# Declaring that operations on the two different banks of a two-bank PSUM tile need not wait for each other

## The chip, the core and the metric

The kernel runs on one core of a Trainium2 chip. The metric is the device time of one execution in microseconds (us). The kernel before was run three times: 1634.38, 1642.93 and 1643.38 us, with a median of 1642.93 us. One further execution was profiled; it took 1644.29 us.

## What is computed

The kernel computes eight batches of sigmoid attention and, on its result, a mixing step and a two-layer network with a ReLU between the layers. Cut to what matters, with B = 8 batches, 12 heads of 64, a sequence of S = 448, d_model = 768 and rank 32:

```python
scores = np.matmul(q, k.transpose(0, 1, 3, 2)) / np.sqrt(64) - np.log(S)
attn = 1.0 / (1.0 + np.exp(-scores))
x = np.matmul(attn, v)                   # heads put side by side: B x S x 768
u = x + (x.transpose(0, 2, 1) @ U @ V).transpose(0, 2, 1)
out = u + np.maximum(u @ w_ch1, 0.0) @ w_ch2
```

The two weight matrices come as 64-bit floating-point numbers and are decoded on the chip.

## The kernel before, in words

**Stages.** A pair of heads at a time, the scores of a pair are computed on TensorE (line L520), put through the sigmoid on ScalarE (L615), split into two float16 parts (L635 on ScalarE, L381 on VectorE) and multiplied by the values (L531, L535); L641 takes the result out of PSUM. Line L381 is a helper (`stt`), so many VectorE operations carry it, those that add a PSUM result to a tile in SBUF among them. After the attention of a batch come the mixing (L686 to L727 for the first two batches, L779 and L788 for the later ones) and the network. Float32 operands are held as two float16 parts, and three products stand for one.

The first four batches go through the network group by group: `ffn_in` computes a chain of 18 matmuls (L861) into one PSUM bank, which ScalarE reads twice (L868 and L869); `ffn_out` computes a chain of 12 matmuls (L881) into another bank, which VectorE adds to a tile in SBUF (L889, shown as L381). While that runs, the attention of the later batches is worked in between. The last four batches go through the network two at a time, by a scheme with seven products of quarter matrices instead of eight (`in_quad`, `out_quad`); its chains of nine matmuls have line L1056, and their banks are read by ScalarE (L1079, L1098) and VectorE (L381). In the profiled execution that last stretch begins at about 1040 us.

**The order.** The kernel does not leave the order of instructions to the compiler. It records its operations in a `Plan`, with an engine, a cost, what they read and write, and a position. `Plan.order` then goes through them as a small simulation and writes down the order in which they are issued; `Plan.emit` issues them in that order, and a manual schedule keeps it. Each engine works through its own list in this order.

**PSUM.** There are eight banks. They are allocated as four tiles of two banks each (`banks0` to `banks3`), because the scores of a pair need two banks that are read by one instruction. Most operations use one bank alone:

```python
for i in range(4):
    t = ps.tile([P, 1024], F32, name=f"banks{i}")
    BANK += [Buffer(t[:, :512]), Buffer(t[:, 512:])]
    TWO.append(Buffer(t.rearrange("p (h s) -> p h s", h=2)))
...
PF, PS_ = [BANK[:4]] + [BANK[:3]] * (B - 1), [BANK[4:]] * 2 + [BANK[3:]] * (B - 2)
```

`PF` are the banks of the network's chains and `PS_` those of the attention and the mixing. From the second pass through the network on (at about 550 us), the network has banks 0, 1 and 2 and the rest has banks 3 to 7, so that the tile `banks1` (banks 2 and 3) belongs half to the one and half to the other. A new user gets the bank of its pool that by the plan has been free for the longest time. The last two stages (`in_quad`, `out_quad`) use four banks at a time out of all eight.

**Waits.** The waits between engines are put in by the framework, from the reads and writes of tiles that it sees. It keeps an instruction that uses one half of a `banks` tile waiting for an earlier instruction of another engine that uses the other half, if one of the two writes. A wait says: this engine's counter has reached this number; so it also waits for all that stands ahead of that number on the other engine.

Of the kernel before, what the change touches and what calls it, by code (L numbers as in the profile page):

```python
# [74 lines left out]
class Buffer:  # L75


    def __init__(self, ap):
        self.ap, self.shares, self.live, self.free = ap, [], False, 0.0


class Tile:
# [11 lines left out]
class Plan:  # L94
# [3 lines left out]


    def __init__(self):  # L100
        self.ops, self.wrote, self.read, self.queues = [], {}, {}, {}

    def tile(self, name, buffers, in_turn=True):
        t = Tile(name, buffers, in_turn)
# [110 lines left out]
                    cand[x[0]].append(u)  # L215
        return done

    def emit(self):
        for i in self.order():
            for t in self.ops[i][7]:  # L220
                assert t.got is not None
            self.ops[i][2]()


@with_exitstack
def fused_kernel(ctx: ExitStack, tc: tile.TileContext, q, k, v, wu, wv, w1, w2, out):
# [82 lines left out]
    for i in range(4):  # L309
        t = ps.tile([P, 1024], F32, name=f"banks{i}")  # L310
        BANK += [Buffer(t[:, :512]), Buffer(t[:, 512:])]
        TWO.append(Buffer(t.rearrange("p (h s) -> p h s", h=2)))
        TWO[-1].shares += BANK[-2:]
        for x in BANK[-2:]:
            x.shares.append(TWO[-1])
# [54 lines left out]
    def pool(cost, fn, reads, writes, pos, after=()):  # L370
        op("POOL", cost, fn, reads, writes, pos, after=after, port=bool(reads))

    def pe(cost, fn, reads, writes, pos, slack=0.8, after=()):
        return op("PE", cost, fn, reads, writes, pos, slack, 0.3, after)

    def ts(eng, out, in_, s1, op0, s2=None, op1=None):
        kw = {} if op1 is None else {"op1": op1}
        eng.tensor_scalar(out=out, in0=in_, scalar1=s1, scalar2=s2, op0=op0, **kw)  # L378

    def stt(out, in0, s, in1, op0, op1):  # L380
        nc.vector.scalar_tensor_tensor(out=out, in0=in0, scalar=s, in1=in1, op0=op0, op1=op1)  # L381

    def scaled(out, in_, s):
        ts(nc.gpsimd, out, in_, s, ALU.mult, 1.0, ALU.mult)

    def rest(out, in_, s, hi):
        stt(out, in_, s, hi, ALU.mult, ALU.subtract)

    def scale_of(parts, kp, n, name, pos, top=TOP):

        e, inv, s = sm(f"e_{name}", n), sm(f"inv_{name}", n), sm(f"s_{name}", n)
        bank = plan.tile("small", PF[0], False)

        def spread():
            for i in range(n):
                nc.tensor.transpose(out=bank.x[:, i * P : (i + 1) * P], in_=parts.x[:, i : i + 1].to_broadcast([P, P]), identity=ident)

        pe(0.11 * n, spread, kp + ["ident"], [bank], pos)
        dve(0.12 + 0.15 * n, lambda: nc.vector.tensor_reduce(  # L399
            out=e.x, in_=bank.x[:, : n * P].rearrange("q (n p) -> q n p", n=n), axis=AX.X, op=ALU.max, apply_absolute_value=True), [bank], [e], pos)  # L400
        dve(0.17, lambda: ts(nc.vector, e.x.bitcast(I32), e.x.bitcast(I32), 0x7F800000, ALU.bitwise_and), [e], [e], pos)
        dve(0.17, lambda: ts(nc.vector, inv.x, e.x, 2.0 ** -100, ALU.max, 1.0 / top, ALU.mult), [e], [inv], pos)
        dve(0.17, lambda: nc.vector.reciprocal(out=s.x, in_=inv.x), [inv], [s], pos)
        return s, inv
# [100 lines left out]
    def scores_of(b, js, products, kp, pos, early):  # L505

        sc = {}
        for j in js:
            if j < 3:
                sc[j] = plan.tile("sc2", TWO if early else TWO[2:], False)  # L510
            else:
                sc[j] = plan.tile("sc", BANK if early else PS_[b][:3] if b >= 2 else PS_[b], False)
        n = 1 if b < WHOLE else 3

        def fn():
            for j in js:
                for i, (x, y) in enumerate(products()):
                    for h in range(2):
                        o = sc[j].x[:, h, :S] if j < 3 else sc[j].x[rows_of(h), :S]
                        nc.tensor.matmul(o, x[rows_of(h), j * P : min(S, j * P + P)], y[rows_of(h)], start=i == 0, stop=i == n - 1)  # L520

        scored.append(pe(len(js) * (4 if b < WHOLE else 3) * MM + 0.2, fn, kp, list(sc.values()), pos, after=values_ops[-2:-1] + scored[-1:]))
        return sc

    def values_of(b, products, tiles, kp, pos):
        av = plan.tile("av", PS_[b], False)

        def fn():
            n = len(products())
            for i, (x, y) in enumerate(products()):  # L530
                nc.tensor.matmul(av.x[:, :S], x[:, 3, :], y(tiles[3], 0), start=i == 0, stop=False, skip_group_check=True)  # L531
            for j in range(3):
                for i, (x, y) in enumerate(products()):
                    for h in range(2):
                        nc.tensor.matmul(  # L535
                            av.x[rows_of(h), :S], x[:, j, rows_of(h)], y(tiles[j], h),
                            start=False, stop=j == 2 and i == n - 1, skip_group_check=True,
                        )

        values_ops.append(pe((16 if b < WHOLE or b in DIRECT else 12) * MM + 0.2, fn, kp, [av], pos))  # L540
        return av
# [115 lines left out]
    def mix(b, pos0, pos1):  # L657
# [18 lines left out]
        for hf in range(2):  # L676
# [3 lines left out]
            for sc in range(4):  # L680
# [2 lines left out]

                def transposes(tr=tr, w=w, sc=sc, hf=hf):
                    for c in range(3):
                        nc.tensor.transpose(  # L686
                            out=tr.x[:w, c * P : (c + 1) * P], in_=u32[hf * 3 + c].x[:, sc * P : sc * P + w], identity=ident
                        )

# [3 lines left out]
                if whole:  # L693
                    def x32(xn=xn, w=w):
                        return xn.x.rearrange("p a b -> p (a b)").bitcast(F32)[:w]

                    act(0.48, lambda tr=tr, w=w, x32=x32: nc.scalar.copy(x32(), tr.x[:w, :384]), [tr], [xn], at)
                    pe(0.66, lambda tp=tp, w=w, sc=sc, x32=x32: nc.tensor.matmul(
                        tp.x[:RANK, :384], uraw[:w, sc], x32(), start=sc == 0, stop=sc == 3), [xn, "uraw"], [tp], at)
                    continue  # L700
                act(0.58, lambda tr=tr, xn=xn, w=w: nc.scalar.activation(xn.x[:w, 0, :], tr.x[:w, :384], AF.Copy, scale=sx.x[:w]),
# [3 lines left out]

                def mixed(xn=xn, w=w, sc=sc, tp=tp):
                    for i, x in enumerate((ua, ub)):
                        nc.tensor.matmul(
                            tp.x[:, :384], x[:w, sc].rearrange("p a b -> p (a b)"), xn.x[:w, i, :],
                            start=sc == 0 and i == 0, stop=sc == 3 and i == 1,  # L710
                        )
# [7 lines left out]
        for c in range(NP):  # L719
            cut = slice(c * P, (c + 1) * P)  # L720
            lp = plan.tile("sc", BANK if b == 0 else PS_[b], False)
            if whole:
                pe(4 * MM, lambda lp=lp, cut=cut: nc.tensor.matmul(lp.x[:, :S], tt.x[:RANK, cut], vraw[:RANK], start=True, stop=True),
                   [(tt, c // 3), "vraw"], [lp], at)
                dve(0.62, lambda lp=lp, c=c: nc.vector.tensor_add(u32[c].x, lp.x[:, :S], u32[c].x), [lp, ku[c]], [ku[c]], at)
            else:
                pe(MM, lambda lp=lp, cut=cut: nc.tensor.matmul(lp.x[:, :S], t16()[:, cut], vst, start=True, stop=True),  # L727
                   [(tt, c // 3), "vst"], [lp], at)
                dve(0.68, lambda lp=lp, c=c: stt(u32[c].x, lp.x[:, :S], kap.x, u32[c].x, ALU.mult, ALU.add),
                    [lp, ku[c], kap], [ku[c]], at)  # L730
# [26 lines left out]
    def mix_half(b, hf, pos):  # L757
# [17 lines left out]
        def mixed():  # L775
            x = xt.x.rearrange("p (c j) d -> p j c d", c=3)
            for j in range(7):
                m = ua[:, j] if j < 3 else ux[:, j - 3]
                nc.tensor.matmul(tp.x[:, :384], m.rearrange("p a b -> p (a b)"), x[:, j], start=j == 0, stop=j == 6)  # L779

        pe(1.2, mixed, [xt, "ux"] + KUA, [tp], pos + 2.0)
        act(0.5, lambda: nc.scalar.activation(tt.x, tp.x[:, :384], AF.Copy, scale=DOWN), [tp], [tt], pos + 2.0)
# [2 lines left out]
        for c in cs:  # L785
            cut = slice((c % 3) * P, (c % 3 + 1) * P)
            lp = plan.tile("sc", PS_[b], False)
            pe(MM, lambda lp=lp, cut=cut: nc.tensor.matmul(lp.x[:, :S], tt.x[:, cut], vst, start=True, stop=True), [tt, "vst"], [lp], at)  # L788
            dve(0.68, lambda lp=lp, c=c: stt(u32[c].x, lp.x[:, :S], kap.x, u32[c].x, ALU.mult, ALU.add), [lp, u32[c], kap], [u32[c]], at)
            largest(lambda c=c: u32[c].x, lambda c=c: mx.x[:, c : c + 1], [u32[c]], (mx, c), at)  # L790
            load(lambda c=c: parked[b][:, c], lambda c=c: u32[c].x, P * S * 4, [u32[c]], [("parked", b, c)], at + 1.0)
# [58 lines left out]
    def ffn_in(b, g, f, pos, banks):  # L850
# [6 lines left out]
        def chain():  # L857
            wx = w.x.rearrange("p x (c f) -> p x c f", c=NP)
            for c in range(NP):
                for i, (x, y) in enumerate(((0, 0), (0, 1), (1, 0))):  # L860
                    nc.tensor.matmul(  # L861
                        ph.x[:, :S], wx[:, x, c, f * P : (f + 1) * P], us.x[:, c, y, :],
                        start=c == 0 and i == 0, stop=c == NP - 1 and i == 2,
                    )
# [8 lines left out]
    def ffn_out(b, g, e, pos, banks):  # L873
# [3 lines left out]
        def chain():  # L877
            wx = w.x.rearrange("p x (c m) -> p x c m", c=FC)
            for f in range(FC):
                for i, (x, y) in enumerate(((0, 0), (0, 1), (1, 0))):  # L880
                    nc.tensor.matmul(  # L881
                        po.x[:, :S], wx[:, x, f, e * P : (e + 1) * P], h.x[:, f, y, :],
                        start=f == 0 and i == 0, stop=f == FC - 1 and i == 2,
                    )
# [167 lines left out]
    def product(bank, wt, n, fs, start, pos, after=()):  # L1052
        def fn():
            for k, f in enumerate(fs):
                for i, (x, y) in enumerate(((0, 0), (0, 1), (1, 0))):
                    nc.tensor.matmul(bank.x[:, :S], wt.x[:, k, FACTOR[n], x], both(f)[:, y],  # L1056
                                     start=start and k == i == 0, stop=k == 2 and i == 2, skip_group_check=True)

        return pe(9 * MM, fn, [wt] + [(f, x) for f in fs for x in range(2)], [bank], pos, 0.3, after)
# [205 lines left out]
            at += STEP  # L1265

    with tc.manual_schedule():
        plan.emit()


# [50 lines left out]
```

## Time and profile before

| | |
|---|---|
| median of three runs | 1642.93 us (1634.38 to 1643.38) |
| profiled execution, time | 1644.29 us |
| its span, from the first to the last instruction | 1642.5 us |
| mean granted TensorE clock | 0.992 |
| TensorE (PE) busy | 1581.4 us, 96% of the span |
| VectorE (DVE) busy | 1089.9 us, 66% |
| ScalarE (ACT) busy | 753.2 us, 46% |
| GpSimd (POOL) busy | 349.3 us, 21% |
| DMA | 302.8 MB, mean 184 GB/s |

The span is the profiler's; the 1.8 us between it and the execution's time lie around it. A row of instructions reads: line, engine, operation, what it writes <- what it reads, count, busy time, mean time of one in ns, and then the idle time of the engine just before them with what ended it. A row of waits reads: engine, tile and line that waited <- engine, tile and line that ended the wait, then the total in us, how many times, and the longest. PEld are the weight loads of TensorE, which overlap its matmuls. Buffer numbers and bank numbers are left out of the names, so that `banks` stands for all eight banks.

### The profile page before, as it was taken

The numbers are of one execution on the slowest core, as the hardware profiler recorded it, in microseconds if no ns is written. First come the engines' busy times: TensorE is split into PE (matmuls) and PEld (weight loads), VectorE is DVE, ScalarE is ACT, GpSimd is POOL, SyncE is SP. The second block draws the span as 40 slices with busy tenths as digits, with TensorE's granted clock in tenths as the row PEclk, the third lists the DMA queues.
The fourth block names the chain that finished last, engine by engine and source line by source line (L and its number), as shares of the span: only waits on it lengthen the run. The fifth ranks groups of instructions, "written<-read, shape, count | busy, mean of one in ns | idle before, by whom it ended". The sixth has DMA issues, their size and how long they took to land.

```text
span 1642.5 us, 23045 instructions
## 1 busy us (share of the span) xinstructions
PE 1581.4 (96%) x8621; PEld 761.8 (46%) x8621; DVE 1089.9 (66%) x1831; ACT 753.2 (46%) x1269; POOL 349.3 (21%) x429
## 2 busy tenths in 40 slices
PE   8999999999999999999999999899999999999998
PEld 3334444444444444444444444445555554545454
DVE  3887885656775566666567688576777577655556
ACT  5565454445565546545746667232323514221210
POOL 0100000005454321111343311045653400000000
PEclk9999999999999999999999999999999999999999
DMA  8688786436667667555565575876773653323321
GB/s 230 210 275 281 205 262 214 159 87 201 202 187 203 195 186 196 152 181 162 172 201 174 177 211 165 244 224 197 248 239 121 235 197 141 134 102 115 120 103 67
DMA packets 204112, 302.80 MB, mean 184 GB/s; under 512 B 124896, under 2 KB 171104, under 8 KB 192736
## 3 DMA queue, kind: packets, MB, share of 16 engines
q1 hardware_dynamic: 204000, 301.34, 58.9%
q8 instruction: 67, 1.10, 0.3%
q14 instruction: 45, 0.37, 0.1%
HBM read 231.11 MB, written 76.04 MB: 187 GB/s over the span
## 4 chain that ended last, share of the span: by engine, by line
PE 84%; DVE 7%; ACT 3%; DMA 3%; SPq 1%; issue 1%; ACTq 0%; DVEq 0%
PE banks L1056 31%; PE banks L881 18%; PE banks L861 18%; PE banks L520 7%; PE banks L535 5%; PE banks L531 2%; DVE stg__108 L381 1%; DMA w<-w_in 1%; PE banks L779 1%; SPq L771 1%; ACT at L615 1%; DVE a L381 0%; DMA w<-parked 0%; DVE w L381 0%; DMA at<-ufar 0%
## 5 line engine op out<-in xcount | busy, mean ns | idle before, releaser
L881 PE MATMUL banks<-h__95,w__93 128*128 128x448 f16 x720 | 145.3, 355 | 6.3 <-ACT h__96 L869 2.5
L881 PE MATMUL banks<-h__96,w__94 128*128 128x448 f16 x720 | 146.6, 356 | 3.8 <-ACT h__95 L869 1.4
L381 DVE SCALAR_TENSOR_TENSOR a<-at,a 128x448 f16<-128x448 f32 (+1 forms) x120 | 120.0, 1024 | 24.8 <-ACT a L635 24.6
L615 ACT ACTIVATE at<-banks,tiny 128x448 f32<-128x448 f32 (+1 forms) x120 | 115.7, 1003 | 39.9 <-DVE a L381 13.6
L881 PEld LDWEIGHTS <-w__93 128*128 128x128 f16 x864 | 82.9, 98 | 93.4 <-issue 21.2
L881 PEld LDWEIGHTS <-w__94 128*128 128x128 f16 x864 | 82.6, 99 | 91.2 <-issue 20.3
L861 PEld LDWEIGHTS <-w__92 128*128 128x128 f16 x864 | 83.5, 98 | 89.0 <-issue 14.5
L861 PEld LDWEIGHTS <-w__91 128*128 128x128 f16 x864 | 83.6, 98 | 84.4 <-issue 8.9
L1056 PEld LDWEIGHTS <-w__91 128*128 128x128 f16 x819 | 80.1, 98 | 82.6 <-issue 5.4
L1056 PEld LDWEIGHTS <-w__93 128*128 128x128 f16 x756 | 74.7, 99 | 79.0 <-issue 12.3
L1056 PEld LDWEIGHTS <-w__92 128*128 128x128 f16 x756 | 73.9, 98 | 72.3 <-issue 3.7
L944 POOL TENSOR_TENSOR w<-w 128x384 f32<-128x384 f32 x96 | 104.7, 1091 | 5.5
L378 POOL TENSOR_SCALAR tiny<-tiny 128x1 f32<-128x1 f32 (+1 forms) x90 | 26.7, 307 | 345.0 <-DVE tiny L378 332.2
L1056 PEld LDWEIGHTS <-w__94 128*128 128x128 f16 x693 | 67.6, 98 | 68.5 <-issue 3.3
L635 ACT ACTIVATE a<-at 128x448 f16<-128x448 f32 (+1 forms) x120 | 97.6, 856 | 1.4 <-PE banks L535 1.1
L861 PE MATMUL banks<-us__89,w__92 128*128 128x448 f16 x432 | 86.9, 356 | 2.8 <-ACT h__96 L869 1.1
L861 PE MATMUL banks<-us__90,w__92 128*128 128x448 f16 x432 | 85.6, 353 | 1.7 <-ACT h__96 L869 1.6
L861 PE MATMUL banks<-us__90,w__91 128*128 128x448 f16 x432 | 85.1, 353 | 2.0 <-DVE tiny L399 1.0
L861 PE MATMUL banks<-us__89,w__91 128*128 128x448 f16 x432 | 85.5, 353 | 0.1
L615 ACT ACTIVATE a<-banks,tiny 128x448 f32<-128x448 f32 (+1 forms) x72 | 62.6, 911 | 27.2 <-PE banks L535 18.5
L940 POOL TENSOR_TENSOR w<-w 128x384 f32<-128x384 f16 x48 | 46.5, 998 | 111.5 <-DVE xnt L948 75.1
L868 ACT ACTIVATE r__98<-banks 128x448 f32<-128x448 f32 x48 | 26.0, 541 | 75.7 <-PE banks L861 43.4
(952 smaller groups left out, 3026.8 us busy)
## 6 DMA issues: line engine op xcount, KB each, us to landing
w<-w_in SPq DMA_DIRECT2D x48, 768.0 KB, 5.6
forms<-xnt SPq DMA_DIRECT2D x24, 768.0 KB, 4.3
w__91<-forms SPq DMA_DIRECT2D x13, 1344.0 KB, 5.7
w__92<-forms SPq DMA_DIRECT2D x12, 1344.0 KB, 5.8
w__93<-forms SPq DMA_DIRECT2D x12, 1344.0 KB, 6.0
w__94<-forms SPq DMA_DIRECT2D x11, 1344.0 KB, 5.7
forms<-scratch SPq DMA_DIRECT2D x144, 96.0 KB, 3.8
w__91<-scratch SPq DMA_DIRECT2D x7, 1536.0 KB, 7.9
```

The source lines that it names most:

```text
L378: eng.tensor_scalar(out=out, in0=in_, scalar1=s1, scalar2=s2, op0=op0, **kw)
L381: nc.vector.scalar_tensor_tensor(out=out, in0=in0, scalar=s, in1=in1, op0=op0, op1=op1)
L520: nc.tensor.matmul(o, x[rows_of(h), j * P : min(S, j * P + P)], y[rows_of(h)], start=i == 0, stop=i == n - 1)
L531: nc.tensor.matmul(av.x[:, :S], x[:, 3, :], y(tiles[3], 0), start=i == 0, stop=False, skip_group_check=True)
L535: nc.tensor.matmul(av.x[rows_of(h), :S], x[:, j, rows_of(h)], y(tiles[j], h), start=False, stop=j == 2 and i == n - 1, skip_group_check=True,)
L615: act(cost, lambda: nc.scalar.activation(out_(), in_(), AF.Sigmoid, bias=bias_s, scale=c if whole else c.x), kin + ["bias"] + kc, kout, pos)
L635: act(0.57 if j == 3 else 0.95, lambda a=a, to=to: nc.scalar.activation(half(a, 0), to.x, AF.Copy, scale=A_UP), kto, [(a, 0)], here + A_OFF)
L861: nc.tensor.matmul(ph.x[:, :S], wx[:, x, c, f * P : (f + 1) * P], us.x[:, c, y, :], start=c == 0 and i == 0, stop=c == NP - 1 and i == 2,)
L881: nc.tensor.matmul(po.x[:, :S], wx[:, x, f, e * P : (e + 1) * P], h.x[:, f, y, :], start=f == 0 and i == 0, stop=f == FC - 1 and i == 2,)
L940: pool(1.0, lambda j=j: nc.gpsimd.tensor_tensor(out=t.x[:, j], in0=quarter(j, 0), in1=quarter(j, 1), op=ALU.add), [(w, j, 0), (w, j, 1)] i ...
L944: pool(1.0, lambda o_=o_, x=x, y=y, sub=sub: nc.gpsimd.tensor_tensor(out=t.x[:, o_], in0=t.x[:, x], in1=t.x[:, y], op=ALU.subtract if sub ...
L1056: nc.tensor.matmul(bank.x[:, :S], wt.x[:, k, FACTOR[n], x], both(f)[:, y], start=start and k == i == 0, stop=k == 2 and i == 2, skip_group ...
```

## The change

The change notes for each of the four tiles which bank a buffer is (`halves`). When an operation is issued, it looks at the last eight operations that used the other bank of its tile. For each of them that runs on another engine, does not itself use both banks, is no dependency that the plan knows of, and shares no SBUF buffer with it, the kernel declares to the framework that no wait is needed between their instructions. An operation that uses both banks is left as it was. So that the instructions are at hand, two helpers (`matmul`, `transpose`) record the matmuls, and `ts`, `stt`, `scaled` and `rest` return what they make.

```diff
 class Buffer:
-        self.ap, self.shares, self.live, self.free = ap, [], False, 0.0
+        self.ap, self.shares, self.live, self.free, self.halves = ap, [], False, 0.0, ()
...
-    def emit(self):
+    def emit(self, tc):
+        recent = {}
         for i in self.order():
             for t in self.ops[i][7]:
                 assert t.got is not None
-            self.ops[i][2]()
+            self.emit_one(i, tc, recent)
+
+    def emit_one(self, i, tc, recent):
+        self.made = []
+        x = self.ops[i][2]()
+        made = self.made + ([] if x is None else [x])
+        eng, deps = self.ops[i][0], set(self.ops[i][3])
+        halves = {h for t in self.ops[i][7] for h in t.got.halves}
+        mine = [t.got for t in self.ops[i][7] if not t.got.halves]
+        for n, side in halves:
+            if (n, 1 - side) in halves:
+                continue
+            for j, old, both, theirs in recent.get((n, 1 - side), ()):
+                if self.ops[j][0] == eng or (n, side) in both or j in deps or any(x is y or y in x.shares for x in mine for y in theirs):
+                    continue
+                for o in old:
+                    for m in made:
+                        tc.declare_no_dep(m.ins, o.ins, reason="the other bank of the tile")
+        for h in halves:
+            recent[h] = recent.get(h, [])[-7:] + [(i, made, halves, mine)]
...
+        BANK[-2].halves, BANK[-1].halves, TWO[-1].halves = ((i, 0),), ((i, 1),), ((i, 0), (i, 1))
...
+    def matmul(*x, **y):
+        plan.made.append(nc.tensor.matmul(*x, **y))
+
+    def transpose(**x):
+        plan.made.append(nc.tensor.transpose(**x))
...
-                nc.tensor.matmul(
+                matmul(
```

No instruction that computes or moves data is added, left out or moved: on each of the five engines the built program has the same instructions in the same order, with other line numbers (matmuls now carry the helpers' lines L395 and L398, the rest stands 27 lines further down). What differs are the waits. On TensorE 948 rows of the listing carry a wait before and 937 now, on VectorE 1419 and 1506, on ScalarE 934 and 943; of these, 374 rows on VectorE name TensorE's counter before and 495 now, and on ScalarE 365 and 413.

One place as an example, at about 921 us of the profile. On TensorE a network chain on a bank of `banks0` is followed by one on a bank of `banks1` (`w10__93` are weights, `h0__95` the hidden layer). Before:

```order
L881 LDWEIGHTS w10__93
L881 MATMUL banks0_110<-h0__95,w10__93 128x448
L881 LDWEIGHTS w10__93
L881 MATMUL banks1_111<-h0__95,w10__93 128x448 [waits Activation_49]
L881 LDWEIGHTS w10__93
```

And now:

```order
L395 LDWEIGHTS w10__93
L395 MATMUL banks0_110<-h0__95,w10__93 128x448
L395 LDWEIGHTS w10__93
L395 MATMUL banks1_111<-h0__95,w10__93 128x448
L395 LDWEIGHTS w10__93
```

The chain on `banks1` no longer waits for ScalarE. On ScalarE, at the same time, the first of the rows takes a hidden layer out of `banks0`; the two L615 rows are sigmoids of scores. Before:

```order
L869 ACTIVATE h1__96<-banks0_110 128x448 [waits PE_49]
L635 ACTIVATE a_99<-at_100 128x896 [waits Activation_49]
L615 ACTIVATE at_100<-banks1_111,tiny_63 128x448
L615 ACTIVATE at_100<-banks3_113,tiny_63 128x896 [waits DVE_49]
L635 ACTIVATE a_99<-at_100 128x448 [waits Activation_49]
```

And now:

```order
L896 ACTIVATE h1__96<-banks0_110 128x448 [waits PE_49]
L662 ACTIVATE a_99<-at_100 128x896 [waits Activation_49]
L642 ACTIVATE at_100<-banks1_111,tiny_63 128x448 [waits PE_49]
L642 ACTIVATE at_100<-banks3_113,tiny_63 128x896 [waits DVE_49,PE_49]
L662 ACTIVATE a_99<-at_100 128x448 [waits Activation_49]
```

The hidden layer's row waits for TensorE in both programs, but before for the counter that the L881 chain on the other bank of `banks0` sets at its end, and now for the earlier one that its own chain sets. The sigmoids were covered by that later number before; now each has a wait of its own.

More of the change, by code (lines that the diff above doesn't have):

```diff
@@ L100, in __init__ @@
     def __init__(self):
-        self.ops, self.wrote, self.read, self.queues = [], {}, {}, {}
+        self.ops, self.wrote, self.read, self.queues, self.made = [], {}, {}, {}, []
     def tile(self, name, buffers, in_turn=True):
@@ L377, in ts @@
         kw = {} if op1 is None else {"op1": op1}
-        eng.tensor_scalar(out=out, in0=in_, scalar1=s1, scalar2=s2, op0=op0, **kw)
+        return eng.tensor_scalar(out=out, in0=in_, scalar1=s1, scalar2=s2, op0=op0, **kw)
     def stt(out, in0, s, in1, op0, op1):
-        nc.vector.scalar_tensor_tensor(out=out, in0=in0, scalar=s, in1=in1, op0=op0, op1=op1)
+        return nc.vector.scalar_tensor_tensor(out=out, in0=in0, scalar=s, in1=in1, op0=op0, op1=op1)
     def scaled(out, in_, s):
-        ts(nc.gpsimd, out, in_, s, ALU.mult, 1.0, ALU.mult)
+        return ts(nc.gpsimd, out, in_, s, ALU.mult, 1.0, ALU.mult)
     def rest(out, in_, s, hi):
-        stt(out, in_, s, hi, ALU.mult, ALU.subtract)
+        return stt(out, in_, s, hi, ALU.mult, ALU.subtract)
     def scale_of(parts, kp, n, name, pos, top=TOP):
@@ L395, in spread @@
             for i in range(n):
-                nc.tensor.transpose(out=bank.x[:, i * P : (i + 1) * P], in_=parts.x[:, i : i + 1].to_broadcast([P, P]), identity=ident)
+                transpose(out=bank.x[:, i * P : (i + 1) * P], in_=parts.x[:, i : i + 1].to_broadcast([P, P]), identity=ident)
         pe(0.11 * n, spread, kp + ["ident"], [bank], pos)
@@ L519, in fn @@
                         o = sc[j].x[:, h, :S] if j < 3 else sc[j].x[rows_of(h), :S]
-                        nc.tensor.matmul(o, x[rows_of(h), j * P : min(S, j * P + P)], y[rows_of(h)], start=i == 0, stop=i == n - 1)
+                        matmul(o, x[rows_of(h), j * P : min(S, j * P + P)], y[rows_of(h)], start=i == 0, stop=i == n - 1)
         scored.append(pe(len(js) * (4 if b < WHOLE else 3) * MM + 0.2, fn, kp, list(sc.values()), pos, after=values_ops[-2:-1] + scored[-1:]))
@@ L530, in fn @@
             for i, (x, y) in enumerate(products()):
-                nc.tensor.matmul(av.x[:, :S], x[:, 3, :], y(tiles[3], 0), start=i == 0, stop=False, skip_group_check=True)
+                matmul(av.x[:, :S], x[:, 3, :], y(tiles[3], 0), start=i == 0, stop=False, skip_group_check=True)
             for j in range(3):
@@ L685, in transposes @@
                     for c in range(3):
-                        nc.tensor.transpose(
+                        transpose(
                             out=tr.x[:w, c * P : (c + 1) * P], in_=u32[hf * 3 + c].x[:, sc * P : sc * P + w], identity=ident
@@ L697, in mix @@
                     act(0.48, lambda tr=tr, w=w, x32=x32: nc.scalar.copy(x32(), tr.x[:w, :384]), [tr], [xn], at)
-                    pe(0.66, lambda tp=tp, w=w, sc=sc, x32=x32: nc.tensor.matmul(
+                    pe(0.66, lambda tp=tp, w=w, sc=sc, x32=x32: matmul(
                         tp.x[:RANK, :384], uraw[:w, sc], x32(), start=sc == 0, stop=sc == 3), [xn, "uraw"], [tp], at)
@@ L707, in mixed @@
                     for i, x in enumerate((ua, ub)):
-                        nc.tensor.matmul(
+                        matmul(
                             tp.x[:, :384], x[:w, sc].rearrange("p a b -> p (a b)"), xn.x[:w, i, :],
@@ L722, in mix @@
             if whole:
-                pe(4 * MM, lambda lp=lp, cut=cut: nc.tensor.matmul(lp.x[:, :S], tt.x[:RANK, cut], vraw[:RANK], start=True, stop=True),
+                pe(4 * MM, lambda lp=lp, cut=cut: matmul(lp.x[:, :S], tt.x[:RANK, cut], vraw[:RANK], start=True, stop=True),
                    [(tt, c // 3), "vraw"], [lp], at)
@@ L726, in mix @@
             else:
-                pe(MM, lambda lp=lp, cut=cut: nc.tensor.matmul(lp.x[:, :S], t16()[:, cut], vst, start=True, stop=True),
+                pe(MM, lambda lp=lp, cut=cut: matmul(lp.x[:, :S], t16()[:, cut], vst, start=True, stop=True),
                    [(tt, c // 3), "vst"], [lp], at)
@@ L778, in mixed @@
                 m = ua[:, j] if j < 3 else ux[:, j - 3]
-                nc.tensor.matmul(tp.x[:, :384], m.rearrange("p a b -> p (a b)"), x[:, j], start=j == 0, stop=j == 6)
+                matmul(tp.x[:, :384], m.rearrange("p a b -> p (a b)"), x[:, j], start=j == 0, stop=j == 6)
         pe(1.2, mixed, [xt, "ux"] + KUA, [tp], pos + 2.0)
@@ L787, in mix_half @@
             lp = plan.tile("sc", PS_[b], False)
-            pe(MM, lambda lp=lp, cut=cut: nc.tensor.matmul(lp.x[:, :S], tt.x[:, cut], vst, start=True, stop=True), [tt, "vst"], [lp], at)
+            pe(MM, lambda lp=lp, cut=cut: matmul(lp.x[:, :S], tt.x[:, cut], vst, start=True, stop=True), [tt, "vst"], [lp], at)
             dve(0.68, lambda lp=lp, c=c: stt(u32[c].x, lp.x[:, :S], kap.x, u32[c].x, ALU.mult, ALU.add), [lp, u32[c], kap], [u32[c]], at)
@@ L860, in chain @@
                 for i, (x, y) in enumerate(((0, 0), (0, 1), (1, 0))):
-                    nc.tensor.matmul(
+                    matmul(
                         ph.x[:, :S], wx[:, x, c, f * P : (f + 1) * P], us.x[:, c, y, :],
@@ L880, in chain @@
                 for i, (x, y) in enumerate(((0, 0), (0, 1), (1, 0))):
-                    nc.tensor.matmul(
+                    matmul(
                         po.x[:, :S], wx[:, x, f, e * P : (e + 1) * P], h.x[:, f, y, :],
@@ L1055, in fn @@
                 for i, (x, y) in enumerate(((0, 0), (0, 1), (1, 0))):
-                    nc.tensor.matmul(bank.x[:, :S], wt.x[:, k, FACTOR[n], x], both(f)[:, y],
+                    matmul(bank.x[:, :S], wt.x[:, k, FACTOR[n], x], both(f)[:, y],
                                      start=start and k == i == 0, stop=k == 2 and i == 2, skip_group_check=True)
@@ L1267, in fused_kernel @@
     with tc.manual_schedule():
-        plan.emit()
+        plan.emit(tc)
 def kernel(**inputs):
```

## The prediction

> **What bounds the kernel now.** I read the busy times first.
>
> ```profile
> span 1642.5 us, 23045 instructions
> PE 1581.4 (96%) x8621; PEld 761.8 (46%) x8621; DVE 1089.9 (66%) x1831; ACT 753.2 (46%) x1269; POOL 349.3 (21%) x429
> ```
>
> TensorE sets the end: it is idle for 1642.5 - 1581.4 = 61.1 us. No change of waits can win more than that and what idleness costs beside it. Next, where the idle time lies: the busy times by stage (first column after the stretch its length, then PE busy with its instructions; the column of 1.00, 0.99 and 0.91 is the granted clock).
>
> ```profile
> 0.00:100.00 100.00, 91.29 (x373) 32.00 (x375) 61.54 (x110) 57.19 (x90) 10.00 (x18) 1.00 0.73 233
> 100.00:550.00 450.00, 443.34 (x2404) 211.79 (x2402) 315.50 (x548) 238.44 (x408) 91.66 (x110) 1.00 0.65 201
> 550.00:1040.00 490.00, 464.42 (x2815) 220.48 (x2814) 325.00 (x557) 290.42 (x487) 128.62 (x187) 0.99 0.63 184
> 1040.00:1100.00 60.00, 52.61 (x251) 25.75 (x252) 41.16 (x68) 18.14 (x31) 10.01 (x9) 0.91 0.74 230
> 1100.00:1640.00 540.00, 529.70 (x2784) 271.79 (x2782) 346.74 (x552) 148.97 (x254) 109.00 (x106) 1.00 0.46 157
> ```
>
> TensorE's gaps are 8.7, 6.7, 25.6, 7.4 and 10.3 us, 58.7 in sum. The third stage has the most; there the network's chains and the attention of later batches share TensorE. Then who ended these gaps, from the waits of TensorE, whose rows sum to 57.0 us in 55 waits:
>
> ```profile
> PE banks L520 <- DMA qk__101<-q_in: 4.2, 1, 4.2
> PE banks L1056 <- DVE us__90 L381: 3.7, 1, 3.7
> PE banks L881 <- ACT at L615: 3.3, 2, 2.1
> PE banks L520 <- ACT at L615: 3.1, 2, 1.9
> PE banks L861 <- ACT h__96 L869: 2.7, 2, 1.6
> PE banks L881 <- ACT h__96 L869: 2.5, 1, 2.5
> PE banks L396 <- ACT r__98 L868: 2.4, 1, 2.4
> PE banks L1056 <- DMA at<-ufar: 2.1, 2, 1.2
> PE banks L1056 <- DMA v__104<-ufar: 2.0, 1, 2.0
> PE banks L520 <- DVE ua__76 L381: 2.0, 1, 2.0
> PE banks L520 <- ACT a L615: 1.9, 2, 1.6
> PE banks L531 <- ACT r__97 L868: 1.6, 1, 1.6
> PE banks L520 <- ACT ub__78 L641: 1.1, 1, 1.1
> PE banks L520 <- DVE stg__108 L381: 0.5, 1, 0.5
> ```
>
> Loads account for 4.2 + 2.1 + 2.0 = 8.3 us. Nearly all the rest are readers of PSUM: TensorE waits to write a bank. Of several the code tells that the bank was not the one read. From 550 us on the network has banks 0 to 2 and the attention banks 3 to 7, so a chain of L881 never writes a bank that a sigmoid (L615) read, nor do L531 and L520 write one that L868 or the network's VectorE addition (`ua__76`) read. These can only be the two halves of `banks1`. Within one pool it is likely, not certain: the plan hands out the bank that has been free longest, so that the latest reader is as a rule the neighbour's.
>
> The same holds in the other direction:
>
> ```profile
> ACT r__98 L868 <- PE banks L881: 21.5, 5, 5.7
> DVE ua__73 L381 <- PE banks L861: 9.8, 5, 4.7
> ```
>
> L868 reads only what L861 made, and the additions of `ua` read only what L881 made. Each waits here for a chain that it doesn't use. How the two directions act together is seen at 921 us, on ScalarE and TensorE:
>
> ```profile
> 921.39 2.44 PE L881 MATMUL banks<-h__95,w__93 128*128 128x448 f16 x12
> 923.87 0.54 ACT L869 ACTIVATE h__96<-banks 128x448 f16<-128x448 f32 x1 [2.74 <-PE banks L881]
> 924.31 0.94 ACT L635 ACTIVATE a<-at 128x896 f16<-128x896 f32 x1
> 925.15 1.71 ACT L615 ACTIVATE at<-banks,tiny 128x448 f32<-128x448 f32 x2
> 925.92 2.43 PE L881 MATMUL banks<-h__95,w__93 128*128 128x448 f16 x12 [2.08 <-ACT at L615]
> ```
>
> ScalarE idles 2.74 us until the L881 chain on the other half of its tile is done, so L635 and the sigmoid behind it are late; and TensorE then idles 2.08 us until that sigmoid has read the other half of the tile that the next chain wants. Two false waits make one gap.
>
> **The change part by part.** It removes waits and moves no work. I sum by stage what goes.
>
> 0 to 100 us: the waits of L520 for L615 and L641, 1.9 + 1.1 = 3.0. The load's 4.2 stays, and so do small waits for data. 100 to 550: of 6.7, 6.0, since one wait there (0.5, for `stg__108`) is for data. 550 to 1040: of 25.6, 23.5; some idle time there has no releaser. 1040 to 1100: of 7.4, 1.5; 4.1 are loads, and the 3.7 for `us__90` is by the code a real one (L1056 adds a second product into the bank that this addition reads); it can only start somewhat earlier. 1100 to 1640: of 10.3, 9.0; the four-bank scheme reuses each bank after its reader, and some real waits remain. Sum: 3.0 + 6.0 + 23.5 + 1.5 + 9.0 = 43.0 us.
>
> A gap costs more than its idle time. A matmul of the long chains takes 352 to 356 ns by itself:
>
> ```profile
> L881 PE MATMUL banks<-h__96,w__93 128*128 128x448 f16 x144 | 28.8, 353 | 0.0
> L1056 PE MATMUL banks<-a,w__92 128*128 128x448 f16 x150 | 33.8, 352 | 0.0
> ```
>
> in a stream one follows another every 529.70 / 2784 = 0.190 us (the last stage). So each gap loses a further 0.353 - 0.190 = 0.163 us in which the array fills again, which the profile counts as busy. The waits of TensorE are 55, of which 4 are for loads; I take 45 as removed: 45 x 0.163 = 7.3, say 7 us.
>
> Third, the clock. These are the stretches at half clock:
>
> ```profile
> 572.60:576.00 3.40, 3.17 (x9) 1.32 (x9) 0.77 (x2) 3.40 (x8) 2.85 (x6) 0.50 0.35 106
> 647.70:651.10 3.40, 3.40 (x19) 1.38 (x18) 1.86 (x4) 2.27 (x4) 1.88 (x5) 0.50 0.99 339
> 678.40:681.80 3.40, 3.40 (x13) 1.17 (x10) 2.97 (x11) 3.33 (x7) 2.62 (x4) 0.50 0.35 116
> 859.30:862.70 3.40, 3.40 (x11) 1.40 (x10) 1.08 (x3) 3.40 (x6) 3.40 (x5) 0.50 0.91 311
> 1040.20:1043.60 3.40, 3.40 (x10) 1.39 (x11) 0.38 (x1) 0.00 (x0) 0.00 (x0) 0.50 0.97 292
> 1084.60:1091.40 6.80, 5.88 (x16) 2.38 (x16) 3.80 (x7) 1.72 (x3) 0.00 (x0) 0.50 0.32 110
> ```
>
> Each follows a wait: the first that for `h__96` (2.5), the second that of L531 (1.6), the third the longest of L520 for L615 (1.9), the fourth that of L396 (2.4), the last two a load (2.0) and `us__90` (3.7). They do not follow every wait; the one at 925 us had none. The first four follow waits that go. At half speed 3.4 us lose 1.7, so I count 4 x 1.7 = 6.8, say 7 us.
>
> [...]
>
> What is added are waits: 495 rows on VectorE name TensorE where 374 did, on ScalarE 413 for 365, some 170 in all, nearly all long since met. Behind each stands the next sigmoid, split or addition of that engine, and behind that TensorE. No row prices one. From below it is nothing, from above the shortest VectorE operation:
>
> ```profile
> L378 DVE TENSOR_SCALAR tiny<-tiny 128x1 int32<-128x1 int32 (+4 forms) x104 | 17.6, 172 | 1.6
> ```
>
> 170 x 0.17 = 29 us. Even that would lie in the idle time of VectorE (553 us of the span) and ScalarE (889 us). I take 0; without that cover it would be up to 29 us.
>
> Sum: 43 + 7 + 7 = 57 us. The profiled execution's own time, 1644.3, becomes 1587; it is 1.4 us over the median of the runs, so I forecast 1586. Behind the waits, TensorE is late next for the loads at 1040 us and for `us__90`.
>
> The bounds. At most all gaps but the loads' go, 58.7 - 8.3 = 50.4, with 51 x 0.163 = 8.3 and all seven half-clock windows, 7 x 1.7 = 11.9: 70.6, which gives 1572. At least three quarters of the sum, 43, which gives 1600.
>
> **The rivals.** *The windows stay.* If the half-clock windows have another cause than these waits, 7 us fall away: 1593. For it speaks that the 925 us gap had none; against it that all follow a wait within the last few us, and that 1100 to 1640, with no wait over 1 us, has clock 1.00 throughout.
>
> *Real waits take the place.* TensorE runs ahead and meets the next true wait: a bank's own reader, a hidden layer, a sigmoid. Then half of the sum returns: 28, 1614. For it: ScalarE works in order, and its sigmoids and hidden layers stand in one queue. Against it: ScalarE and VectorE lose false waits too, and have idle time in every stage.
>
> *No effect.* The counters already passed may cover most of what is declared, as the numbers of waits on TensorE (948 before, 937 now) suggest: 1643. Against it stands the place at 921 us, where the wait is gone.
>
> *Slower.* TensorE writes one half while ScalarE or VectorE reads the other, which the waits forbade, and such matmuls run slower. The readers are busy for
>
> ```profile
> L615 ACT ACTIVATE at<-banks,tiny 128x448 f32<-128x448 f32 (+1 forms) x120 | 115.7, 1003 | 39.9 <-DVE a L381 13.6 <-PE banks L520 12.2 <-PE banks L881 5.7
> L868 ACT ACTIVATE r__98<-banks 128x448 f32<-128x448 f32 x48 | 26.0, 541 | 75.7 <-PE banks L861 43.4 <-PE banks L881 21.5 <-PE banks L520 3.9
> L381 DVE SCALAR_TENSOR_TENSOR ub__82<-banks,tiny,ub__82 128x448 f32<-128x448 f32 x29 | 19.7, 680 | 28.0 <-PE banks L861 9.8 <-PE banks L1056 9.7 <-PE banks L881 3.0
> ```
>
> and their likes, by my estimate 500 us, with the neighbour written in half of that, 250 us. The gain would be eaten at 57 / 250 = 23% slower matmuls; at 35% the time is 1643 - 57 + 88 = 1674. Against it: matmuls beside readers of other tiles keep their 352 ns in stages with much and with little ScalarE work (the L881 and L1056 rows).
>
> [...]
>
> **How the numbers follow.** The forecast 0.58 (1572 to 1600); windows stay 0.14; real waits 0.16; no effect 0.06; slower 0.06. Faster by over 1%, about what a measurement of this kernel can tell from no change, that is below 1627: 0.58 + 0.14 + 0.16 = 0.88; same 0.06, slower 0.06. The range reaches from 1572 to the rival of the real waits, 1614.
>
> **What would show it.** Right: the waits of TensorE fall from 57 us to about 14, the idle time from 61 to about 18; rows such as L868 waiting for the chains of the second layer disappear; half-clock windows remain only near 1040 to 1090 us and the mean clock rises; PE busy falls by about 14 us. Windows elsewhere would speak for the first rival; new waits of TensorE for readers with as many us for the second; waits as before for the third; a matmul mean above 356 ns for the fourth. The forecast is wrong if the time is above 1614 or below 1572.

## The result, and the profile after

| | before | after |
|---|---|---|
| median of the runs | 1640.41 us (1634.38 to 1643.38) | 1582.18 us (1580.85 to 1585.82) |
| profiled execution, its span | 1644.29, 1642.5 us | 1585.82, 1584.0 us |
| mean granted TensorE clock in it | 0.992 | 0.997 |

The ratio of after to before is 0.9653, with a 95% interval of 0.9618 to 0.9688: 58 us less by the medians. (Before was run once more beside the changed kernel, hence a median other than the 1642.93 above.)

The busy times of the changed kernel:

```profile
span 1584.0 us, 23059 instructions
PE 1566.2 (99%) x8621; PEld 760.2 (48%) x8621; DVE 1093.3 (69%) x1831; ACT 755.3 (48%) x1269; POOL 341.2 (22%) x429
```

TensorE idles 17.8 us instead of 61.1 and is busy 15.2 us less for the same 8621 matmuls. So of the 58.5 us that the span lost, 43.3 are idle time, and 15.2 are busy time that the same matmuls no longer take. By stage, with the later boundaries moved forward by what was won until then:

```profile
0.00:100.00 100.00, 93.33 (x377) 33.20 (x379) 61.14 (x109) 56.41 (x88) 11.69 (x18) 0.97 0.72 232
100.00:550.00 450.00, 448.71 (x2451) 214.94 (x2448) 323.57 (x563) 246.30 (x422) 91.36 (x112) 1.00 0.68 206
550.00:990.00 440.00, 438.08 (x2703) 209.84 (x2701) 313.39 (x530) 281.69 (x471) 118.95 (x184) 1.00 0.69 194
990.00:1045.00 55.00, 50.68 (x267) 25.49 (x266) 36.01 (x71) 16.57 (x31) 7.67 (x8) 0.97 0.86 253
1045.00:1580.00 535.00, 535.00 (x2830) 276.71 (x2828) 358.55 (x562) 154.30 (x261) 111.52 (x108) 1.00 0.48 163
```

The gaps are now 6.7, 1.3, 1.9, 4.3 and 0.0 us. The middle stage, which had 25.6, has nearly none, and in the last stage TensorE is never idle. The complete list of TensorE's waits (L395 are all matmuls, L398 all transposes; the lines of readers have moved down by 27):

```profile
PE banks L395 <- DMA qk__101<-q_in: 4.2, 1, 4.2
PE banks L398 <- DVE ua__72 L752: 2.4, 1, 2.4
PE banks L395 <- DMA at<-ufar: 2.0, 3, 1.0
PE banks L395 <- DMA v__104<-ufar: 2.0, 1, 2.0
PE banks L395 <- ACT h__95 L896: 1.2, 1, 1.2
PE banks L398 <- DVE tiny L825: 0.9, 1, 0.9
PE banks L395 <- ACT at L642: 0.6, 1, 0.6
PE banks L398 <- ACT xnt L728: 0.3, 1, 0.3
PE banks L395 <- DMA a<-ufar: 0.3, 1, 0.3
```

13.9 us in 11 waits, where there were 57.0 in 55. More than half, 8.5 us, are the loads. The place that the prediction showed at 921 us, ScalarE first, now reads:

```profile
885.16 1.10 ACT L642 ACTIVATE at<-banks,tiny 128x896 f32<-128x896 f32 x1 [1.75 <-DVE a L408]
886.16 0.53 ACT L896 ACTIVATE h__96<-banks 128x448 f16<-128x448 f32 x1
886.58 0.95 ACT L662 ACTIVATE a<-at 128x896 f16<-128x896 f32 x1
887.42 1.72 ACT L642 ACTIVATE at<-banks,tiny 128x448 f32<-128x448 f32 x2
886.91 4.71 PE L395 MATMUL banks<-h__95,w__93 128*128 128x448 f16 x24
```

The hidden layer (L896) follows the sigmoid before it without the 2.74 us, and the two chains of the second layer on TensorE have become one piece of 24 matmuls, with no gap of 2.08 us.

### The profile page after: what moved, and what is told of

It is laid out like the page before. It is cut to its first block, busy times and chain, and to the rows that moved or that the text cites. A ratio compares the mean times of both kernels' runs of the same rounds, so it can differ in the third digit from the quotient of the medians.

```text
span 1584.0 us, 23059 instructions
## 1 busy us (share of the span) xinstructions
PE 1566.2 (99%) x8621; PEld 760.2 (48%) x8621; DVE 1093.3 (69%) x1831; ACT 755.3 (48%) x1269; POOL 341.2 (22%) x429
## 4 chain that ended last, share of the span: by engine, by line
PE 91%; DMA 4%; DVE 3%; ACT 1%; SPq 1%; issue 1%; POOL 0%; DVEq 0%; ACTq 0%
PE banks L395 90%; DMA w<-w_in 1%; DMA v__104<-v_in 1%; PE banks L398 1%; DVE stg__109 L408 0%; DMA w<-parked 0%; DVE a L408 0%; DMA qk__102<-ufar 0%; DMA at<-ufar 0%; DVE tiny L465 0%; ACT at L642 0%; DVE at L408 0%; DMA qk__103<-q_in 0%; DMA a<-ufar 0%; SPq L798 0%
## 5 line engine op out<-in xcount | busy, mean ns | idle before, releaser
L395 PEld LDWEIGHTS <-w__91 128*128 128x128 f16 x1683 | 163.4, 98 | 163.0 <-issue 12.1
L395 PEld LDWEIGHTS <-w__93 128*128 128x128 f16 x1620 | 156.3, 98 | 154.0 <-issue 12.1
L395 PEld LDWEIGHTS <-w__92 128*128 128x128 f16 x1620 | 157.1, 98 | 151.8 <-issue 7.3
L395 PEld LDWEIGHTS <-w__94 128*128 128x128 f16 x1557 | 150.1, 98 | 149.5 <-issue 14.0
L395 PE MATMUL banks<-h__96,w__94 128*128 128x448 f16 x753 | 152.5, 353 | 1.2 <-ACT h__95 L896 1.2
L395 PE MATMUL banks<-h__95,w__93 128*128 128x448 f16 x762 | 153.7, 353 | 0.0
L395 PE MATMUL banks<-us__89,w__91 128*128 128x448 f16 x492 | 99.5, 353 | 0.0
L395 PE MATMUL banks<-us__90,w__91 128*128 128x448 f16 x492 | 99.4, 353 | 0.0
L395 PE MATMUL banks<-us__89,w__92 128*128 128x448 f16 x489 | 99.2, 353 | 0.0
L395 PE MATMUL banks<-us__90,w__92 128*128 128x448 f16 x489 | 99.0, 353 | 0.0
L642 ACT ACTIVATE a<-banks,tiny 128x448 f32<-128x448 f32 (+1 forms) x72 | 62.8, 910 | 21.1 <-PE banks L395 18.2
L895 ACT ACTIVATE r__97<-banks 128x448 f32<-128x448 f32 x48 | 25.9, 540 | 71.2 <-PE banks L395 69.6
L895 ACT ACTIVATE r__98<-banks 128x448 f32<-128x448 f32 x48 | 25.9, 540 | 69.5 <-PE banks L395 69.3
L395 PEld LDWEIGHTS <-stg__108 64*128 64x128 f16 (+3 forms) x675 | 32.6, 102 | 43.1 <-issue 23.1
L395 PEld LDWEIGHTS <-stg__109 64*128 64x128 f16 (+3 forms) x675 | 32.3, 102 | 43.4 <-issue 23.9
L974 ACT CAST xnt<-w 128x1536 f16<-128x1536 f32 x24 | 35.2, 1467 | 32.5 <-POOL w L971 31.9
```

The source lines that it names most:

```text
L395: plan.made.append(nc.tensor.matmul(*x, **y))
L642: act(cost, lambda: nc.scalar.activation(out_(), in_(), AF.Sigmoid, bias=bias_s, scale=c if whole else c.x), kin + ["bias"] + kc, kout, pos)
L895: act(0.54, lambda: nc.scalar.activation(r.x, ph.x[:, :S], AF.Relu, scale=DOWN_H), [ph], [r], pos - EV_IN)
L974: act(1.45, lambda: nc.scalar.copy(o.x[:, :, :, 0], t.x.rearrange(order)), [(t, j) for j in range(4)], [(o, 0)], pos)
```

## The experiments

All use the changed kernel and alter only for which pairs of operations the declaration is made, but for the last. Each was timed beside the kernel before on the same chip, whose median was 1638.07 us for the first four and 1641.36 us for the last three; the ratios are to these.

**The two directions.** The theory: a gap is made of two false waits in a row, a reader that starts late because it waits for a chain on the other bank, and a chain that waits for that reader. The rivals: TensorE's own waits are the whole cost, or the two directions have gaps of their own.

TensorE's side alone:

```diff
-            if (n, 1 - side) in halves:
+            if (n, 1 - side) in halves or eng != "PE":
```

> Declares only where the later operation is TensorE's: TensorE need not wait for a reader of the other bank, but ScalarE and VectorE still wait for TensorE's writes to the other bank. Theory (a gap is made of two false waits, the reader that starts late and the chain that waits for it, and either end of it can break most of a gap): the readers stay late, so TensorE still meets real waits for late sigmoids and hidden layers; rather more than half of the 58 us, 1600 to 1612 us, with 15 to 30 us of TensorE's waits left. Rival A (TensorE's own waits are the whole cost, the readers' waits are covered): as with the whole change, 1580 to 1590. Rival B (the two directions each have their own gaps, and share the gain): 1605 to 1618, and the two halves add up to the whole.

Measured: 1604.25 us, ratio 0.9789 (0.9774 to 0.9803), 2.1% less. The readers' side alone:

```diff
-            if (n, 1 - side) in halves:
+            if (n, 1 - side) in halves or eng == "PE":
```

> Declares only where the later operation is a reader (ScalarE, VectorE): these need not wait for TensorE's writes to the other bank, but TensorE still waits for readers of the other bank. Theory (either end breaks most of a gap): with the readers on time, the waits that TensorE keeps are mostly over when it comes to them; most of the gain, 1583 to 1595 us, and together with the TensorE half well over the whole 58 us. Rival A (TensorE's own waits are the cost): little, over 1625. Rival B (the directions share the gain): 1608 to 1620, adding up to the whole.

Measured: 1591.16 us, ratio 0.9708 (0.9691 to 0.9725), 2.9% less. Together the halves make 5.0%, the whole change 3.5%. So they don't have separate gaps, and TensorE's waits are not the whole: each side alone breaks more than half of the gaps (TensorE idles 32.6 and 22.2 us, against 61.1 before and 17.8 with both), and the readers' side breaks more. Why, the same place shows. With TensorE's side alone:

```profile
896.33 4.71 PE L395 MATMUL banks<-h__95,w__93 128*128 128x448 f16 x24
898.81 0.54 ACT L896 ACTIVATE h__96<-banks 128x448 f16<-128x448 f32 x1 [3.13 <-PE banks L395]
```

The gap of TensorE is gone (24 matmuls in one piece), but ScalarE still idles 3.13 us for a bank that it doesn't read. With the readers' side alone:

```profile
891.48 0.54 ACT L896 ACTIVATE h__96<-banks 128x448 f16<-128x448 f32 x1
892.23 4.71 PE L395 MATMUL banks<-h__95,w__93 128*128 128x448 f16 x24
```

ScalarE is on time, and TensorE has no gap here either, though it still has its wait: the reader is done before TensorE comes to it. What is left shows the difference. Three of the longest waits of TensorE that the first kernel keeps, and then those of the second, besides loads:

```profile
PE banks L395 <- ACT at L642: 4.0, 3, 1.9
PE banks L395 <- DVE us__90 L408: 2.9, 1, 2.9
PE banks L395 <- ACT h__95 L896: 1.7, 1, 1.7
```

```profile
PE banks L395 <- ACT r__97 L895: 4.0, 1, 4.0
PE banks L395 <- DVE w L408: 2.0, 1, 2.0
PE banks L398 <- DVE ua__72 L752: 1.4, 1, 1.4
```

In all, loads included, the first has 28.6 us in 27 waits, the second 18.2 in 12: where readers start late, TensorE meets many of them.

**The tiles.** The tile `banks1` alone, and the three others:

```diff
-            if (n, 1 - side) in halves:
+            if (n, 1 - side) in halves or n != 1:
```

```diff
-            if (n, 1 - side) in halves:
+            if (n, 1 - side) in halves or n == 1:
```

> Declares only for the tile banks1, which from the second pass on belongs half to the network and half to the attention. Theory (false waits arise in every tile, also inside one pool): less than half of the gain, 18 to 25 us, 1616 to 1623. Rival (what costs is the tile that two pools share, so that the network waits for the attention): more than half, 1590 to 1610.

> Declares for the tiles banks0, banks2 and banks3 and not for banks1. Theory (every tile): 40 to 48 us of gain, 1592 to 1600, and with the run for banks1 alone somewhat over the whole 58 us. Rival (the shared tile): little gain, 1610 to 1630.

Measured: 1618.54 us, ratio 0.9873 (0.9858 to 0.9888), and 1594.32 us, ratio 0.9727 (0.9712 to 0.9743). The tile that the network and the attention share from 550 us on gives 1.3%, the three others 2.7%. The stage that begins there, with `banks1` alone and then with the three others:

```profile
550.00:1020.00 470.00, 452.57 (x2777) 216.67 (x2776) 321.61 (x546) 287.99 (x482) 129.31 (x185) 1.00 0.66 189
550.00:995.00 445.00, 437.83 (x2684) 209.00 (x2683) 311.99 (x526) 281.18 (x471) 126.76 (x184) 0.99 0.67 190
```

TensorE's gaps there, 25.6 us before, are 17.4 and 7.2. So most of the cost comes from the other tiles, whose two banks the same kind of work uses in turn. For those the prediction had only the plan's rule, that the bank free longest is taken; the times are in line with it.

**The stages, and the clock.** The change without the middle stage, and in it alone (`self.mid` is true from the 41st chain of the first layer to the first product of the last scheme):

```diff
-            if (n, 1 - side) in halves:
+            if (n, 1 - side) in halves or self.mid:
```

```diff
-            if (n, 1 - side) in halves:
+            if (n, 1 - side) in halves or not self.mid:
```

> The change everywhere but in the middle stage, from the second pass of the network (about 540 us) to the first product of the last scheme (about 1030 us), which keeps all its waits. Theory (the middle stage holds 23.5 of the 43 us of gaps and the four half-clock stretches that go, which come from its gaps): the gain falls from 58 to 22 to 28 us, 1610 to 1616, with stretches at half clock again between 540 and 1030 us. Rival A (the half-clock stretches have another cause, so that they also stay away here): 7 us less time and no such stretch in the middle stage, 1603 to 1608. Rival B (real waits made up for part, the middle stage is worth less than its gaps): below 1603.

> The change in the middle stage alone. Theory (the stages add up): a gain of 30 to 36 us, 1602 to 1608, together with the run without the middle 54 to 62 us; no stretch at half clock left in the middle stage except after loads. Rival (what is won early only moves the wait to the next stage, so that stages do not add up): the sum of the two runs differs from the whole by over 10 us.

Measured: 1611.30 us, ratio 0.9815 (0.9789 to 0.9840), and 1607.50 us, ratio 0.9797 (0.9774 to 0.9819). Without the middle stage its gaps return; the other kernel has them not, but has those of the last stage:

```profile
550.00:1000.00 450.00, 425.97 (x2573) 202.82 (x2572) 296.18 (x503) 269.64 (x455) 128.10 (x184) 0.98 0.63 179
```

```profile
550.00:1000.00 450.00, 449.16 (x2771) 215.60 (x2769) 316.70 (x541) 286.42 (x480) 117.87 (x186) 1.00 0.69 195
1100.00:1575.00 475.00, 466.94 (x2455) 239.75 (x2454) 306.06 (x490) 138.13 (x237) 85.65 (x83) 1.00 0.46 156
```

24.0 us of gaps in the first kernel's middle stage, 0.8 in the second's. The two gains, 1.85% and 2.03%, make 3.9% against 3.5% of the whole, 0.4% or 6.7 us over; the intervals of the two are 0.25% each way, so that the stages add up as far as can be told. By the medians the gains are 30.1 us, a little over the 22 to 28 that were expected, and 33.9 us; their sum, 63.9 us, is a little over the expected 54 to 62.

The half-clock stretches came back in the kernel that keeps the middle stage's waits: at 567.4, 642.5, 673.3 and 919.0 us, four as before. So they come from the gaps, and the rival that gave them another cause fell. But a gap is not enough: the kernel with `banks1` alone keeps 17.4 us of gaps between 550 and 1020 us and has no half-clock stretch there (the mean clock of its profiled execution is 0.999). Nor are the four at the same gaps as before. Two stretches (cells) of 3.41 us of this kernel, each with the one behind it:

```profile
850.75:854.16 3.41, 1.62 (x9) 0.94 (x10) 3.31 (x8) 3.09 (x5) 0.84 (x1) 1.00 0.77 236
854.16:857.58 3.42, 3.42 (x22) 1.64 (x21) 0.92 (x3) 3.42 (x6) 3.42 (x5) 1.00 0.97 302
915.60:919.01 3.41, 1.33 (x8) 0.61 (x7) 1.08 (x2) 2.27 (x4) 0.00 (x0) 1.00 0.95 350
919.01:922.43 3.42, 3.42 (x11) 1.38 (x10) 3.42 (x5) 3.25 (x7) 0.00 (x0) 0.50 0.61 223
```

In the kernel before, the gap that lies at 852 here had half clock behind it (859.3) and the one at 919 here had none (925 there). Now it is the other way round. The last section has what the traces show of it.

**A version that might beat both.** The longest wait that is left besides the first load is one of TensorE at 55 us, for an addition (L752, `ua__72`) that stands in VectorE's queue behind a decoding that waits for a load. The plan counts 2.0 us for such a load to land; the profile shows 5.2. So:

```diff
-                 6.0 * n - 150.0 if g == i == 0 else pos + n)
+                 6.0 * n - 150.0 if g == i == 0 else pos + n, 5.0 if g == 0 else 2.0)
```

> The whole change, and in the plan the loads of the first weight group are given 5.0 us to land instead of 2.0 (the profile shows 5.2), so that VectorE has the first batch's additions ahead of the decoding that waits for such a load; the order of many operations moves. Theory (the 2.4 us wait of TensorE for an addition at 55 us and the two stretches at half clock behind it, 6.8 us at half speed, come from that place in VectorE's queue): 3 to 6 us faster than the change, 1576 to 1579. Rival (the plan's other moves cost as much, or the wait goes to another place): within 2 us of the change or slower, 1580 to 1588.

Measured: 1583.71 us, ratio 0.9649 (0.9629 to 0.9670): the same as the change's 0.9653. The rival held. The wait at 55 us is gone, and another has come:

```profile
85.14 1.85 PE L395 MATMUL banks<-qk__101 64*128 64x448 f32 x4 [2.98 <-ACT a L642]
```

with half clock behind it from 85.2 us (the mean clock from 0 to 100 us is 0.98). The wait went to another place. No version was found that is faster than the change.

## Why the prediction was right

The forecast was 1586 us, 57 less than its median of before; it became 1582, 58 less. By its own steps:

*The gaps.* Forecast to go: 3.0, 6.0, 23.5, 1.5 and 9.0 us, 43.0 in sum. Gone by the two stage tables: 2.0, 5.4, 23.7, 3.1 and 10.3, 44.5 in sum. The middle stage was right to 0.2 us. In the first stage less went, since a wait grew: that for `ua__72` was 0.8 us before and is 2.4 now. TensorE comes there at 53.0 us instead of 54.1, and the addition still stands behind a decoding that waits for a load, which is the second rival in small. In the last two stages more went than was thought, and one step there was wrong: the 3.7 us wait for `us__90` was kept in the sum, in a stage of which only 1.5 us were to go. It is real, as the code says, but it is not in the list any more. VectorE's chain of operations up to that addition is now done when TensorE comes. Two of its rows and GpSimd's before, and the same now:

```profile
1074.50 0.68 DVE L381 SCALAR_TENSOR_TENSOR stg__108<-banks,tiny,us__89 128x448 f32<-128x448 f32 x1 [1.41 <-PE banks L1056]
1078.36 1.33 DVE L381 SCALAR_TENSOR_TENSOR w<-h__95,us__89 128x448 f32<-128x448 f32 x1
1074.85 4.35 POOL L940 TENSOR_TENSOR w<-w 128x384 f32<-128x384 f16 x4 [36.47 <-DMA w<-scratch]
```

```profile
1033.53 0.68 DVE L408 SCALAR_TENSOR_TENSOR stg__108<-banks,tiny,us__89 128x448 f32<-128x448 f32 x1
1036.12 0.61 DVE L408 SCALAR_TENSOR_TENSOR w<-h__95,us__89 128x448 f32<-128x448 f32 x1
1037.81 4.29 POOL L967 TENSOR_TENSOR w<-w 128x384 f32<-128x384 f16 x4 [37.44 <-DMA w<-scratch]
```

VectorE lost a false wait of 1.41 us ahead of the chain. Besides, six of its operations that touch no PSUM, of which `w` is one, took 0.8 to 1.4 us while GpSimd was at work and take 0.1 to 0.6 now that GpSimd starts later: 4.4 us together. With TensorE's side alone the wait for `us__90` still costs 2.9; with the readers' side alone it is gone, although three of these operations still take 1.33 us. So a real wait too can be there partly because of false ones ahead of it; how much of the 3.7 us the later start of GpSimd takes away is not shown.

*The refilling and the clock.* Forecast 7 + 7, seen as PE busy falling by 14; it fell by 15.2. 44 waits fewer at 0.163 us are 7.2. The half-clock stretches were six, seven cells of 3.4 us in all; now there are

```profile
54.80:61.60 6.80, 6.20 (x16) 2.07 (x16) 6.70 (x18) 0.94 (x2) 1.92 (x3) 0.50 0.66 242
1003.75:1007.10 3.35, 3.09 (x10) 1.42 (x10) 0.68 (x1) 0.00 (x0) 0.00 (x0) 0.50 0.93 299
```

three cells, so four fewer, 6.8 us, as forecast; but not the same ones. The pair behind the `us__90` wait went with it, and a new pair came behind the `ua__72` wait, at a place where by the prediction's own signs a window spoke for its first rival. That the number was right was in part luck. The half-clock time differs between executions of one kernel, too: among the 14 timed executions of the kernel before beside the experiments, those with a mean clock of 0.997 or 0.998 took 1636.72 to 1637.64 us and those with 0.994 took 1641.59 to 1644.22 us. The profiled one had 0.992, so its seven cells, from which the term of 7 us was read, are more than usual. The 0.163 us is an estimate of the prediction, and no run shows by itself what a gap costs beside its length. The place of the example agrees with it: the two chains are busy 2.44 and 2.43 us with the gap between them and 4.71 us in one piece, 0.16 us less, with matmul ends that the profile models. 7.2 + 6.8 leaves 1.2 us of the 15.2 unexplained.

*The added waits.* Costed at nothing, with VectorE's and ScalarE's idle time as cover. The last stage, where TensorE has no gap at all with the added waits in place, shows that the cover held there.

*The rivals.* Real waits took the place of false ones in the amount of a few us, not of half: of the 13.9 us of waits that are left, 5.4 are not for loads. That matmuls slow down beside a reader of the neighbouring bank is not seen: the groups of the changed kernel, which for the first time may write beside it, are not slower than the 353 to 356 ns of before.

```profile
L395 PE MATMUL banks<-h__96,w__94 128*128 128x448 f16 x753 | 152.5, 353 | 1.2 <-ACT h__95 L896 1.2
```

Such a mean takes in matmuls with and without a reader beside them. The place of the example has one with, in the kernel with TensorE's side alone:

```profile
900.09 1.71 ACT L642 ACTIVATE at<-banks,tiny 128x448 f32<-128x448 f32 x2
```

The first of these two sigmoids (0.72 us of the 1.71) reads one half of `banks1`, while the second of the two chains (898.6 to 901.0 us) writes the other half. With the readers' side alone, and in the changed kernel, that sigmoid is done before the second chain begins. The 24 matmuls take 4.71 us in all three.

What the prediction did not see is the share of the two directions. It priced the gaps by TensorE's list of waits and took the readers' waits as a cause behind them; that the readers' side alone would give 2.9 of the 3.5% did not come out of its sum.

## What to carry to other kernels

A framework that keeps order by tile sees one tile where this kernel uses two PSUM banks apart; here it took 3.5% off the time to declare needless the waits that came of it. Where a wait's releaser can't have touched the waiter's data, as when a reader of one chain waits for another chain, look at what they share; and look at the evicting engines' waits, not only at TensorE's: taking the false waits from the readers alone gave most of the gain (2.9 of the 3.5%). In this kernel a gap of TensorE cost its length, by the prediction's estimate (0.353 - 0.190 us) about 0.16 us more, and at times 3.4 us at a clock of 0.50 behind it, by half the speed 1.7 us.

## What the runs showed of the hardware

In these traces the half clock goes with how long TensorE idles within one cell, a stretch of 3.413 us, and not with the length of a gap. The cells come from the records of the clock: those at 0.50 in the kernel before, up to TensorE's last matmul, last 3.413 us, and the last of them 6.827; they start at 572.58 us and 22, 31, 84, 137 and 150 times 3.413 us later. The two of the changed kernel start 278 times 3.413 us from each other, the four of the kernel without the middle stage 22, 31 and 103 times after the first. The first microseconds of the traces have no record of the clock (12.8 us of the kernel before, 10.5 of the changed kernel) and are left out here.

Counted over the nine traces, with the cells of each laid by its own half-clock stretches, every cell in which TensorE idled 1.84 us or more was followed by one at half clock (26 cells), and of the cells with less, 26 with 1.37 to 1.83 us were not. In the kernel before and the changed kernel alone these are 8 cells with 1.87 to 2.74 us and 8 with 1.37 to 1.77. There are four exceptions. One cell with 1.44 us was followed by half clock, at 52 us of the kernel with the readers' side alone. And three times the half clock stayed for a second cell, though TensorE idled only 0.55 to 0.94 us in the first: at 1084 us of the kernel before (0.94), at 55 us of the changed kernel (0.55) and at 84 us of the kernel with TensorE's side alone. What decides these four is open. A cell of the kernel before, followed by the 0.50 shown in the prediction:

```profile
569.20:572.60 3.40, 1.16 (x7) 0.49 (x5) 1.20 (x2) 1.41 (x4) 3.12 (x5) 1.00 0.87 260
```

Two cells with nearly the same idle time, each with its next, of the kernel with `banks1` alone (1.83 us idle) and of the kernel with the middle stage alone (1.84 us):

```profile
660.67:664.09 3.42, 1.59 (x9) 0.60 (x7) 3.42 (x5) 1.20 (x2) 0.00 (x0) 1.00 0.23 67
664.09:667.50 3.41, 3.18 (x22) 1.54 (x23) 3.38 (x12) 3.34 (x6) 1.72 (x4) 1.00 0.54 144
```

```profile
81.08:84.49 3.41, 1.57 (x8) 0.60 (x8) 2.12 (x4) 3.41 (x6) 0.09 (x1) 1.00 0.98 404
84.49:87.90 3.41, 3.41 (x12) 1.11 (x9) 3.41 (x7) 2.02 (x4) 0.00 (x0) 0.50 0.48 147
```

So in the kernel without the middle stage a gap of 2.39 us, of which 1.79 us lie in one cell, has a clock of 1.00 behind it (852 us above), and a shorter one of 2.08 us, which lies in one cell, has 0.50 (919 us above), for 3.4 us. At 0.50 matmuls took longer: in the changed kernel 14 float32 matmuls of 128x448 took 6.15 us at 55.9 us, where at 47.6 us, at 1.00, they took 3.42. In the last pair shown the 1.84 us are two short gaps in one cell, of 0.76 and 1.08 us. This was read from gaps that the kernels happened to have; no run made a gap of a chosen length at a chosen place.
